# Agent attention with a gated convolution on one core: output rows issued by GpSimd in place of SyncE

## The chip, the core and the metric

The kernel runs on one core of one Trainium2 chip. The metric is the device time of one execution in microseconds, here the median of several runs. The core has five engines that run their own instruction queues: TensorE (PE; its weight loads are PEld), VectorE (DVE), ScalarE (ACT), GpSimd (POOL) and SyncE (SP). A queue runs in order: an instruction that waits holds everything behind it on its engine. Transfers are issued by an instruction on some engine's queue and then run on 16 DMA engines.

## The reference

Two stages, batch 4, sequence 12800, width 128, 49 agents:

```python
def sm(a, b):
    s = scale * (a @ b.transpose(0, 2, 1))
    s = s - s.max(-1, keepdims=True)
    e = np.exp(s)
    return e / (e.sum(-1, keepdims=True) + 1e-09)
a2k = sm(agents, k)
agent_v = a2k @ v
q2a = sm(q, agents)
x = q2a @ agent_v
# then, over the sequence
gate_pre = sum(conv_w[k] * xp[:, k:k + S, :] for k in range(5))   # xp: x, 4 zeros ahead
gate = 1.0 / (1.0 + np.exp(-gate_pre))
out = gate * (x @ w_val) @ w_out
```

## The kernel before

**Tiling.** Each batch of 12800 positions is cut into ten units of 1280 and 25 chunks of 512. A unit of k, q or v is loaded into one of eleven buffers `ld`. A unit of k gives agent scores (`key_scores`, L367 on PE), copied to `ks` by ScalarE; their maximum goes over VectorE. A unit of v gives exponentials (L459, ACT), a transpose (L377, DVE) and the accumulation `av` (L467, PE). When a batch is through, `fold_weights` turns `av` and the weights into the matrices `stat` and `wo16`, in steps on VectorE (`den`, `avT`, `mx`, `rs`, `wst`), GpSimd (`gw`, L517) and PE (L612 and others). So attention output is never formed by itself: the query side makes the softmax over agents, and the folded matrices do the rest.

**The query side.** `queries` takes a unit of q: scores on PE in one of two banks `sc`, transpose `sT` and maximum `qmx` on VectorE, subtraction `qw` on GpSimd (L703), exponential on ScalarE (L711), sums `qsm`, `qr` and product `qw` on VectorE (L716 to L725), then `pt`, the high and low halves, on ScalarE (L732) and GpSimd (L737, L747). SyncE then issues a DMA transpose of `pt` into the rows `x` (L788), and two copies that shift rows for the convolution (L837). GpSimd copies the last four columns of a segment into the next one (`halo`, L772), which has to wait for the transposes.

**The chunk.** For chunk t: `gates` (L875, L879 on PE, then tanh `th` on ACT, L888), `values` (L902, L906 on PE, `h` on DVE L915, the half-precision `hh` on ACT L921, the rest `hl` on GpSimd L926), and two chunks later `project` (L945 to L947 on PE, the copy `ob` on ACT L959). Each pair of chunks fills one of three buffers `ob` of 128 x 1024, and is sent out by one transfer (L974, SyncE). There are 53 such transfers: 48 of 512 KB, 3 of 256 KB (the last chunk of the first three batches) and 2 of 128 KB, since the very last chunk is cut in two.

**The order.** Every step is given to `Plan.add` with an engine, a time in us, what it reads and what it writes. `Plan.order` plays this through: PE keeps the order written, each other engine takes the ready step with the longest tail behind it, and the issues are written out in the order of their planned starts. Transfers ("dma") are one queue, SyncE's, and may have eight in flight (`lanes`). So a step's engine and planned time change the places of other steps too.

Of the kernel before, what the change touches and what calls it, by code (L numbers as in the profile page):

```python
# [66 lines left out]
class Plan:  # L67
# [11 lines left out]
    def add(self, engine, us, fn, reads=(), writes=(), moved=0.0, key=None, urge=0.0):  # L79
        i = len(self.steps)  # L80
        need = set()
        for x in reads:
            need |= self.wrote.get(x, set())
        for x in writes:
            need |= self.wrote.get(x, set()) | self.read.get(x, set())
        for x in reads:
            self.read.setdefault(x, set()).add(i)
        for x in writes:
            self.wrote[x], self.read[x] = {i}, set()
        self.steps.append((engine, us, fn, need, moved, key))  # L90
        self.urge.append(urge)

    def order(self):
        n = len(self.steps)
        after = [[] for _ in range(n)]
        last = None
        for i, (engine, us, fn, need, moved, key) in enumerate(self.steps):
            for j in need:
                after[j].append(i)
            if engine == "pe":  # L100
                if last is not None and last not in need:
                    after[last].append(i)
                last = i
        tail = [0.0] * n
        for i in reversed(range(n)):
            engine, us, fn, need, moved, key = self.steps[i]
            cost = us + HOP + (moved + LAND if moved else 0.0)
            if engine == "pe":
                cost = us
            tail[i] = cost + self.urge[i] + max((tail[j] for j in after[i]), default=0.0)  # L110
        engines = ("pe", "act", "dve", "pool", "dma")
        free = dict.fromkeys(engines, 0.0)
        wire = 0.0
        lanes = [0.0] * LANES
        left = [len(s[3]) for s in self.steps]
        at = [0.0] * n
        queues = {e: [] for e in engines}
        pe = [i for i, s in enumerate(self.steps) if s[0] == "pe"]
        here = 0
        for i, s in enumerate(self.steps):  # L120
            if s[0] != "pe" and not left[i]:
                queues[s[0]].append(i)
        start = [0.0] * n
        kind = None
        done = 0
        while done < n:
            best = None
            free["dma"] = max(free["dma"], wire - BACKLOG, lanes[0])
            for e in engines:
                if e == "pe":  # L130
                    if here < len(pe) and not left[pe[here]]:
                        pick, when = pe[here], max(free[e], at[pe[here]])
                    else:
                        continue
                elif queues[e]:
                    q = queues[e]
                    soon = min(max(free[e], at[i]) for i in q)
                    open_ = [i for i in q if at[i] <= soon + 0.05]
                    pick = max(open_, key=lambda i: (tail[i], -i))
                    for i in q:  # L140
                        if tail[i] > tail[pick] + 1.0 and at[i] < soon + 0.6 * self.steps[pick][1]:
                            pick = i
                    when = max(free[e], at[pick])
                else:
                    continue
                if best is None or when < best[0]:
                    best = when, e, pick
            when, e, i = best
            engine, us, fn, need, moved, key = self.steps[i]
            if e == "pe":  # L150
                here += 1
                if key != kind:
                    when += 0.12
                kind = key
            else:
                queues[e].remove(i)
            start[i] = when
            free[e] = when + us
            end = when + us + HOP
            if moved:  # L160
                wire = max(wire, when + 0.5) + moved
                end = max(wire, when + us) + LAND
                lanes = lanes[1:] + [end]
            done += 1
            for j in after[i]:
                if i in self.steps[j][3]:
                    left[j] -= 1
                    at[j] = max(at[j], end)
                    if not left[j] and self.steps[j][0] != "pe":
                        queues[self.steps[j][0]].append(j)  # L170
        self.start = start
        return sorted(range(n), key=lambda i: (start[i], i))
# [3 lines left out]
def tile_agent_attention_gated_conv(  # L176
# [9 lines left out]
    nc = tc.nc  # L186
# [61 lines left out]
    def bank():  # L248
        turn[0] += 1
        i = turn[0] % 2  # L250
        return sc[i], ("sc", i)
# [680 lines left out]
    def project(t):  # L932
        b, n0, w = chunks[t]
        x = b % 2
        wo16, oscale = wo16s[x], oscales[x]
        hh, hl = hhs[t % 3][:, 0:w], hls[t % 3][:, 0:w]
        if t >= NT - 2:
            ps, at_p = bank()
            po = ps[:, 0, 0:w]
        else:  # L940
            po, at_p = outp[:, 0:w], "out"
        scale = w / CH

        def matmuls():
            nc.tensor.matmul(out=po, lhsT=wo16[:, 0, :], rhs=hh, start=True, stop=False)  # L945
            nc.tensor.matmul(out=po, lhsT=wo16[:, 1, :], rhs=hh, start=False, stop=False)  # L946
            nc.tensor.matmul(out=po, lhsT=wo16[:, 0, :], rhs=hl, start=False, stop=True)  # L947

        add(
            "pe", 0.65 * scale, matmuls, [("hh", t % 3), ("hl", t % 3), ("wo16", x)], [at_p],  # L950
            key="c",
        )
        g = t if w == CH else NT - 1
        pair = (t // NCH * 13 + t % NCH // 2) if t < NT - 1 else (B - 1) * 13 + 12
        o = (n0 // CH % 2) * CH if w == CH else n0 - (N - CH)
        ob = obs[pair % NOB]
        add(
            "act", 0.16 + 0.46 * scale,
            lambda: nc.scalar.activation(  # L959
                out=ob[:, o : o + w], in_=po, func=AF.Copy, scale=oscale  # L960
            ),
            [at_p, ("oscale", x)], [("ob", pair % NOB, o)],
        )
        single = w < CH or n0 + w == N
        if single:
            lo, keys = o, [("ob", pair % NOB, o)]
        elif o:
            lo, keys = 0, [("ob", pair % NOB, 0), ("ob", pair % NOB, CH)]
        else:
            return  # L970
        n = o + w - lo
        add(
            "dma", 0.48,
            lambda: nc.sync.dma_start(  # L974
                out=outT[b, :, n0 + w - n : n0 + w], in_=ob[:, lo : lo + n]
            ),
            keys, [], n * 0.00125,
        )
# [61 lines left out]
    def gate_and_state(t):  # L1040
# [3 lines left out]
        "k": key_scores, "v": agent_values, "q": queries, "t": transposes,  # L1044
        "max": lambda b: step(key_max, b), "fold": lambda b: step(fold_weights, b),
        "g": gate_and_state, "a": values, "o": project,
    }
    ahead, done = 0, 0
# [56 lines left out]
```

## Time and profile before

| | |
|---|---|
| median of 3 runs | 433.42 us (433.0 to 433.8) |
| the profiled execution's own time | 432.69 us |
| its span, first to last instruction | 430.8 us |
| mean granted TensorE clock | 0.994 |
| busy: PE, DVE, ACT, POOL | 401.8, 299.0, 300.0, 227.3 us |
| bytes moved by DMA | 127.55 MB, 296 GB/s |
| read from and written to HBM | 79.25 MB, 26.21 MB |

Busy time leaves out register, branch, semaphore and transfer-issuing instructions. A row of waits has the engine and line that waited, what released it, us in total, times, and the longest. A row of the chain has start, length, and what ran. A row of the timeline has start, length, engine, line, what was done, and in brackets how long the engine stood idle before it and who ended that. Rows of "SPq" are SyncE's queue.

### The profile page before, as it was taken

How to read it: one execution, taken by the hardware profiler on the slowest of the kernel's cores; microseconds unless marked ns; L12 is line 12 of the kernel's file. 1: busy time of each engine (PE TensorE's matmuls, PEld its weight loads, DVE VectorE, ACT ScalarE, POOL GpSimd, SP SyncE). 2: the span in 40 equal slices, each digit the busy share in tenths (PEclk: the TensorE clock that was granted, in tenths of full speed). 3: DMA queues.
4: the chain of work that ended last, by engine and by line, in shares of the span. 5: the costliest groups of instructions: out<-in, count | busy, mean ns of one | idle time of the engine just before them, and what ended most of it. 6: DMA issues, size and time to landing. Idle time of an engine off the chain costs nothing.

```text
span 430.8 us, 8867 instructions
## 1 busy us (share of the span) xinstructions
PE 401.8 (93%) x3307; PEld 194.8 (45%) x3307; DVE 299.0 (69%) x567; ACT 300.0 (70%) x520; POOL 227.3 (53%) x258
## 2 busy tenths in 40 slices
PE   3878888999999999999999999999999999999995
PEld 1347333335555444444555543435555544434442
DVE  3676879877686887678666886677667787566231
ACT  2474436678986577778876676768886667777875
POOL 1002246664466765544467664662366566777543
PEclk9999989999999999999999999999999999999999
DMA  8999999999999999999999999999999996554633
GB/s 293 422 417 414 369 387 331 287 339 315 311 332 313 288 312 314 351 302 341 367 299 389 288 299 276 350 273 300 341 373 336 217 206 190 149 136 158 209 127 123
DMA packets 75365, 127.55 MB, mean 296 GB/s; under 512 B 50962, under 2 KB 51218, under 8 KB 75324
## 3 DMA queue, kind: packets, MB, share of 16 engines
q1 hardware_dynamic: 75324, 127.00, 95.6%
q8 instruction: 26, 0.43, 0.4%
q14 instruction: 15, 0.12, 0.1%
HBM read 79.25 MB, written 26.21 MB: 245 GB/s over the span
## 4 chain that ended last, share of the span: by engine, by line
PE 69%; DVE 12%; DMA 9%; ACT 5%; issue 3%; POOL 1%; SPq 0%; DVEq 0%; POOLq 0%; ACTq 0%
PE gate L875 21%; PE sc L367 14%; PE av L467 8%; PE val L902 4%; PE val L906 4%; PE gate L879 4%; PE out L945 4%; PE out L946 4%; PE out L947 4%; DMA ld<-qT 3%; DMA ld<-vP 3%; DVE h L915 2%; DMA x<-pt 2%; ACT e L459 2%; ACT th L888 1%
## 5 line engine op out<-in xcount | busy, mean ns | idle before, releaser
L926 POOL TENSOR_TENSOR hl<-h,hh 128x512 f16<-128x512 f32 (+1 forms) x101 | 117.4, 1164 | 112.6 <-ACT hh L921 111.7
L875 PE MATMUL gate<-x,stat 128*128 128x512 f16 (+1 forms) x500 | 124.2, 378 | 3.2 <-ACT th L888 3.2
L915 DVE SCALAR_TENSOR_TENSOR h<-th,val 128x512 f32<-128x512 f32 x100 | 67.7, 677 | 68.0 <-PE out L946 44.5
L367 PE MATMUL sc<-ld,ag_sb 128*32 128x320 f32 x1280 | 101.3, 448 | 10.7 <-DMA ld<-kT 8.4
L888 ACT ACTIVATE th<-gate,unscale 128x512 f32<-128x512 f32 x100 | 68.3, 683 | 22.5 <-PE gate L879 20.7
L959 ACT ACTIVATE ob<-out,oscale 128x512 f32<-128x512 f32 x98 | 67.2, 686 | 18.7 <-PE out L947 18.5
L875 PEld LDWEIGHTS <-stat 128*128 128x128 f16 x505 | 45.7, 97 | 66.3 <-issue 18.1
L921 ACT CAST hh<-h 128x512 f16<-128x512 f32 (+1 forms) x101 | 61.5, 609 | 12.8 <-DVE h L915 12.0
L703 POOL TENSOR_TENSOR qw<-sT,qmx 128x490 f32<-128x490 f32 x40 | 41.9, 1047 | 45.5 <-DVE qmx L698 45.4
L367 PEld LDWEIGHTS sc<-ld,ag_sb 128*32 128x32 f32 x1280 | 36.8, 111 | 63.5 <-issue 25.4
L393 ACT COPY ks<-sc 128x640 f32<-128x640 f32 x40 | 27.7, 692 | 35.7 <-PE sc L367 33.4
L467 PE MATMUL av<-ld,eT 128*64 128x129 f32 x800 | 49.5, 275 | 2.1 <-DMA ld<-vP 1.8
L747 POOL TENSOR_TENSOR pt<-qw,pt 128x490 f16<-128x490 f32 x40 | 44.5, 1115 | 11.8 <-ACT pt L732 11.6
L467 PEld LDWEIGHTS av<-ld,eT 128*64 128x64 f32 x800 | 43.8, 136 | 12.2 <-issue 7.2
L459 ACT ACTIVATE e<-ks,kbias 128x320 f32<-128x320 f32 x80 | 39.1, 553 | 6.5 <-DVE kbias L448 3.2
L377 DVE STREAM_TRANSPOSE eT<-e 128x640 f32<-128x640 f32 x40 | 33.6, 842 | 11.5 <-ACT e L459 5.3
L377 DVE STREAM_TRANSPOSE sT<-sc 128x640 f32<-128x640 f32 x40 | 33.4, 835 | 10.6 <-PE sc L367 10.4
L402 DVE TENSOR_REDUCE kmx<-ks 128x2 f32<-128x640 f32 x39 | 31.5, 816 | 12.0 <-ACT ks L393 12.0
L879 PE MATMUL gate<-x,stat 95*128 95x512 f16 x100 | 38.0, 380 | 0.0
L902 PE MATMUL val<-x,stat 128*128 128x512 f16 x100 | 37.8, 378 | 0.1
L906 PE MATMUL val<-x,stat 95*128 95x512 f16 x100 | 37.8, 378 | 0.0
L945 PE MATMUL out<-hh,wo 128*128 128x512 f16 x98 | 37.2, 379 | 0.0
(127 smaller groups left out, 397.2 us busy)
## 6 DMA issues: line engine op xcount, KB each, us to landing
ld<-vP SPq DMA_DIRECT2D x40, 645.0 KB
ld<-kT SPq DMA_DIRECT2D x40, 640.0 KB
ld<-qT SPq DMA_DIRECT2D x40, 640.0 KB
outT<-ob SPq DMA_DIRECT2D x48, 512.0 KB
x<-x SPq DMA_DIRECT2D x18, 375.0 KB
x<-x SPq DMA_DIRECT2D x18, 100.0 KB
outT<-ob SPq DMA_DIRECT2D x3, 256.0 KB
x<-x SPq DMA_DIRECT2D x4, 187.5 KB
```

Of the source, the lines that this page charges most:

```text
L367: nc.tensor.matmul(out=out[g * BLK : (g + 1) * BLK, j, 0:GT], lhsT=ag_sb[:, b, j * BLK : (j + 1) * BLK], rhs=src[:, g * GT : (g + 1) * GT] ...
L377: nc.vector.transpose(out=out.rearrange("p n (j i) -> p j n i", j=2), in_=in_.rearrange("p j (n i) -> p j n i", i=BLK),)
L467: nc.tensor.matmul(out=av[o : o + AP_, 0 : C + 1], lhsT=et[:, n, :], rhs=vt[:, n, :], start=(u == 0 and n < 2), stop=(u == NU - 1 and n >= ...
L875: nc.tensor.matmul(out=pg, lhsT=stat[:, k, :], rhs=x1[:, c : c + w], start=(k == 0), stop=False,)
L879: nc.tensor.matmul(out=pg, lhsT=stat[0 : TAPS * X2R, TAPS + 1, :], rhs=x2[0 : TAPS * X2R, o2 : o2 + w], start=False, stop=True,)
L888: lambda: nc.scalar.activation(out=th, in_=pg, func=AF.Tanh, scale=unscale[:, 0:1]),
L902: nc.tensor.matmul(out=pv, lhsT=stat[:, TAPS, :], rhs=x1s[(b * NCH + n0 // CH) // 5 % NX][:, PAD + o2 : PAD + o2 + w], start=True, stop=False,
L906: nc.tensor.matmul(out=pv, lhsT=stat[0 : TAPS * X2R, TAPS + 2, :], rhs=x2[0 : TAPS * X2R, o2 : o2 + w], start=False, stop=True,)
L915: lambda: nc.vector.scalar_tensor_tensor(out=h, in0=th, scalar=1.0, in1=pv, op0=ALU.add, op1=ALU.mult),
L921: "act", 0.16 + 0.42 * scale, lambda: nc.scalar.copy(out=hh, in_=h),
L926: lambda: nc.gpsimd.tensor_tensor(out=hl, in0=h, in1=hh, op=ALU.subtract),
L959: lambda: nc.scalar.activation(out=ob[:, o : o + w], in_=po, func=AF.Copy, scale=oscale),
```

## The change

The output transfer of `project` becomes a step of GpSimd with a planned time of 1.0 us, issued from GpSimd's queue. In `Plan.order` only SyncE's transfers take one of the eight places in flight.

```diff
@@ Plan.order
             if moved:
                 wire = max(wire, when + 0.5) + moved
                 end = max(wire, when + us) + LAND
-                lanes = lanes[1:] + [end]
+                if e == "dma":
+                    lanes = lanes[1:] + [end]
@@ project
         add(
-            "dma", 0.48,
-            lambda: nc.sync.dma_start(
+            "pool", 1.0,
+            lambda: nc.gpsimd.dma_start(
                 out=outT[b, :, n0 + w - n : n0 + w], in_=ob[:, lo : lo + n]
             ),
             keys, [], n * 0.00125,
```

The lines below the first hunk have numbers one higher in the changed kernel (L926 is L927 there, and so on). PE's order is the same; the orders of the others move. SyncE's queue loses its 53 output rows, and GpSimd's gains them. Three places follow.

GpSimd at the end of the program, before (`hl` are the low halves of the last chunks):

```order
L926 TENSOR_TENSOR hl_118<-h_112,hh_115 128x512
L926 TENSOR_TENSOR hl_116<-h_110,hh_113 128x512
L926 TENSOR_TENSOR hl_117<-h_111,hh_114 128x512
L926 TENSOR_TENSOR hl_118<-h_112,hh_115 128x512
L926 TENSOR_TENSOR hl_116<-h_110,hh_113 128x256
L926 TENSOR_TENSOR hl_117<-h_111,hh_114 128x256
```

and with the change:

```order
L927 TENSOR_TENSOR hl_117<-h_111,hh_114 128x512
L927 TENSOR_TENSOR hl_118<-h_112,hh_115 128x512
L975 DMA outT<-ob_120 128x1024
L927 TENSOR_TENSOR hl_116<-h_110,hh_113 128x256
L927 TENSOR_TENSOR hl_117<-h_111,hh_114 128x256
L975 DMA outT<-ob_121 128x1024
L975 DMA outT<-ob_119 128x256 x2
```

The last three transfers stand behind both of the last low halves.

VectorE in the weight fold of the second batch, before (`avT`, `mx`, `rs`, `wst` are the fold's steps, `sT` is the transpose of the next unit's scores out of the bank `sc`):

```order
L532 RECIPROCAL rs<-mx 128x1
L725 TENSOR_TENSOR qw_90<-qw_90,qr_95 128x490
L915 SCALAR_TENSOR_TENSOR h_110<-th_107,val 128x512
L583 TENSOR_SCALAR wst_123<-gw,rs 128x5x49
L564 TENSOR_REDUCE mx<-av 128x1
L568 TENSOR_SCALAR mx<-mx 128x1
L572 RECIPROCAL rs<-mx 128x1
L573 TENSOR_SCALAR wst_123<-av,rs 128x49
L558 SCALAR_TENSOR_TENSOR wst_123<-av,rs,wst_123 128x30
L558 SCALAR_TENSOR_TENSOR wst_123<-av,rs,wst_123 128x15
L558 SCALAR_TENSOR_TENSOR wst_123<-av,rs,wst_123 128x4
L377 STREAM_TRANSPOSE sT_85<-sc_133 128x2x10x32
```

and with the change:

```order
L533 RECIPROCAL rs<-mx 128x1
L584 TENSOR_SCALAR wst_123<-gw,rs 128x5x49
L916 SCALAR_TENSOR_TENSOR h_110<-th_107,val 128x512
L559 SCALAR_TENSOR_TENSOR wst_123<-gw,rs,wst_123 128x5x15 x3
L559 SCALAR_TENSOR_TENSOR wst_123<-gw,rs,wst_123 128x5x4
L378 STREAM_TRANSPOSE sT_85<-sc_133 128x2x10x32
```

The product `qw_90` and its sums went behind the transpose, and so did five short steps of the fold; the four products from `gw` went ahead of it. GpSimd's `gw` now stands ahead of a low half and not behind it. The fold of the third batch moves in the same way.

GpSimd after the fold of the third batch, before (`x_2<-x_1` is the halo copy, `qw_90<-sT_86` the subtraction of the next unit):

```order
L926 TENSOR_TENSOR hl_118<-h_112,hh_115 128x512
L737 TENSOR_SCALAR pt_96<-qw_89 128x10x30
L926 TENSOR_TENSOR hl_116<-h_110,hh_113 128x512
L747 TENSOR_TENSOR pt_96<-qw_89,pt_96 128x10x49
L926 TENSOR_TENSOR hl_117<-h_111,hh_114 128x512
L772 COPY x_2_101<-x_1_100 128x4
L703 TENSOR_TENSOR qw_90<-sT_86,qmx_88 128x490
L926 TENSOR_TENSOR hl_118<-h_112,hh_115 128x512
```

and with the change:

```order
L927 TENSOR_TENSOR hl_116<-h_110,hh_113 128x512
L975 DMA outT<-ob_121 128x1024
L927 TENSOR_TENSOR hl_117<-h_111,hh_114 128x512
L748 TENSOR_TENSOR pt_96<-qw_89,pt_96 128x10x49
L704 TENSOR_TENSOR qw_90<-sT_86,qmx_88 128x490
L738 TENSOR_SCALAR pt_96<-qw_89 128x10x30
L773 COPY x_2_101<-x_1_100 128x4
L975 DMA outT<-ob_119 128x1024
L927 TENSOR_TENSOR hl_118<-h_112,hh_115 128x512
```

The subtraction stands ahead of the halo copy now; an output and the low half stand behind it.

## Prediction

> **What bounds the kernel now.** I read the page first, then PE's waits, then a table of busy time by stage, then the chain and the timeline at the places that the table points to. The page's head and two of its engine rows:
>
> ```profile
> span 430.8 us, 8867 instructions
> ...
> PE 401.8 (93%) x3307; PEld 194.8 (45%) x3307; DVE 299.0 (69%) x567; ACT 300.0 (70%) x520; POOL 227.3 (53%) x258
> ```
>
> TensorE is busy for 401.8 of 430.8 us, so everything that this change could ever win lies in the 29.0 us in which it is idle. The table by stage (start and end, length, busy time and instruction count of PE, PEld, DVE, ACT, POOL, then clock, DMA share, GB/s) shows where those are:
>
> ```profile
> 0.00:45.00 45.00, 32.23 (x426) 19.35 (x426) 28.19 (x59) 20.28 (x36) 5.35 (x15) 1.00 0.97 388
> 45.00:75.00 30.00, 24.70 (x233) 10.83 (x237) 25.48 (x57) 16.26 (x29) 13.45 (x17) 0.94 1.02 358
> 90.00:143.00 53.00, 52.71 (x451) 27.85 (x450) 37.81 (x63) 40.88 (x75) 32.63 (x36) 1.00 1.06 315
> 143.00:150.00 7.00, 6.08 (x57) 3.10 (x56) 6.62 (x22) 5.34 (x10) 4.54 (x6) 1.00 0.98 335
> 242.00:250.00 8.00, 7.08 (x70) 3.54 (x68) 7.62 (x24) 5.50 (x10) 5.00 (x7) 1.00 1.03 377
> 253.00:267.00 14.00, 13.03 (x99) 5.79 (x97) 10.53 (x23) 9.61 (x18) 6.48 (x7) 1.00 1.08 310
> 384.00:421.00 37.00, 36.99 (x181) 16.19 (x179) 15.39 (x25) 29.64 (x49) 22.93 (x24) 1.00 0.51 166
> ```
>
> Before 75 us TensorE idles 12.77 + 5.30 = 18.07 us, and there is no output row to send yet. From 90 us on it stands at full use (52.71 of 53, 36.99 of 37) but for short gaps: 0.92 us at 143 to 150, 0.92 at 242 to 250, 0.97 at 253 to 267. Its waits name who ends them:
>
> ```profile
> PE gate L875 <- ACT th L888: 3.2, 6, 1.0
> PE sc L367 <- DVE sT L377: 2.1, 3, 0.9
> ```
>
> These two are the only kinds that recur after 75 us; none of PE's waits there is for a load or an output. The transfers that move cost SyncE this much (first the waits of its queue: us in total, times, longest; then the instructions: ns least, median, most):
>
> ```profile
> SPq L974 <- ACT ob L959: 43.3, 22, 4.4
> ...
> L974 SPq DMA_DIRECT2D outT<-ob x53: 332/401/1497, 75.6 to 427.1; - x53
> ...
> L788 SPq DMA_TRANSPOSE x<-pt x36: 1342/3943/7002, 76.2 to 400.6; - x36
> ```
>
> **Part 1: SyncE is relieved.** It loses 53 issues of 0.40 us, about 21 us, and 43.3 us of waiting for the output copies. That is off the path: TensorE does not wait for SyncE in any stage after 75 us, save through one chain, here with its start and length:
>
> ```profile
> 253.32 9.10 DMA x<-pt
> ...
> 262.84 0.19 POOL x L772
> 263.02 0.99 POOL qw L703
> ...
> 264.55 0.68 ACT th L888
> ...
> 265.27 1.24 PE gate L875 x5
> ```
>
> A DMA transpose lands late; the four-column halo copy on GpSimd waits for it; a softmax subtraction stands behind the copy, its exponential holds ScalarE, the tanh behind it is late, and TensorE loses the 0.97 us of that stage. In the changed order the subtraction goes ahead of the copy (the piece of GpSimd's order shown above), and SyncE no longer has an output between its loads there. The transpose itself comes later, since its softmax was pushed back. So the stall can go whole (−0.97) or stay (0); I take half, **−0.5**. What is late next there is the low half behind the copy, which has some slack (below).
>
> **Part 2: VectorE's order at the weight folds.** The planner gives the folds of the second and third batch another order. Rows of the first, before:
>
> ```profile
> 145.00 0.21 DVE L512 TENSOR_TENSOR avT<-av,den 128x49 f32<-128x49 f32 x1
> ...
> 146.25 1.03 POOL L517 TENSOR_TENSOR gw<-avT,moe_sb 128x245 f32<-128x245 f32 x1
> ...
> 146.74 0.68 DVE L915 SCALAR_TENSOR_TENSOR h<-th,val 128x512 f32<-128x512 f32 x1
> 147.34 0.46 DVE L583 TENSOR_SCALAR wst<-gw,rs 128x245 f16<-128x245 f32 x1
> ...
> 149.07 0.84 DVE L377 STREAM_TRANSPOSE sT<-sc 128x640 f32<-128x640 f32 x1
> 149.84 1.27 DVE L558 SCALAR_TENSOR_TENSOR wst<-gw,rs,wst 128x75 f16<-128x75 f32 x4
> ...
> 149.97 1.28 PE L367 MATMUL sc<-ld,ag_sb 128*32 128x320 f32 x16 [0.92 <-DVE sT L377]
> ```
>
> TensorE waits 0.92 us for the transpose of the scores, which frees its bank. In the new order gw follows at once on avT (145.2, to 146.27), wst takes 0.46 (to 146.75), h 0.68 (to 147.43), four products of L558 1.27 (to 148.70), and the transpose starts there in place of 149.07: 0.4 us earlier. Twice, **−0.8**. It is gone if L558 meets a low half on GpSimd, as both read two inputs from the same memory; then 0.
>
> **Part 3: GpSimd issues.** The trace has no issue by GpSimd, so I bound its price c. The same transfer takes SyncE 0.33 to 1.50 us, and the far row is the DMA transpose, 3.94 us. The nearest by engine are GpSimd's own passes over 128 partitions (xcount, busy, mean ns, idle before):
>
> ```profile
> L926 POOL TENSOR_TENSOR hl<-h,hh 128x512 f16<-128x512 f32 (+1 forms) x101 | 117.4, 1164 | 112.6 <-ACT hh L921 111.7
> ...
> L703 POOL TENSOR_TENSOR qw<-sT,qmx 128x490 f32<-128x490 f32 x40 | 41.9, 1047 | 45.5 <-DVE qmx L698 45.4
> ```
>
> I take c = 1.1 us, between these two means; the planner books 1.0. A gain below SyncE's 0.33 is excluded, as the work is not less. The SBUF — State Buffer page of the Trainium skill, section "A bandwidth-pool intuition that's wrong", has 620 ns for a DMA that GpSimd issues alone and about 3100 ns when a VectorE copy holds their common port. By the first figure the tail below would cost an estimated 0.4 us in place of 1.8 and the sum would be 432.2 on the profiled run; no run here shows either yet.
>
> 53 issues at 1.1 add 58 us to GpSimd, 227 to 285 of 431: it does not become the bound, but it has deadlines. In the last stretch:
>
> ```profile
> 419.09 0.69 ACT L959 ACTIVATE ob<-out,oscale 128x512 f32<-128x512 f32 x1 [0.34 <-PE out L947]
> ...
> 420.36 1.15 POOL L926 TENSOR_TENSOR hl<-h,hh 128x512 f16<-128x512 f32 x1 [1.23 <-ACT hh L921]
> ...
> 422.64 0.38 PE L947 MATMUL out<-hl,wo 128*128 128x512 f16 x1
> ```
>
> The output copy ends at 419.78, the issue would hold GpSimd to 420.88, and the low half behind it would end at 422.04 in place of 421.51; its product is due at 422.64. So an issue may take 0.6 us more, c up to 1.7, before TensorE waits. In the dense stages the softmax steps queue behind the issues; the tanh steps there already wait 3.2 us in six places, and I add **+0.4** (none to 1.0, a second such stall like that at 253) for issues that come in at a bad moment.
>
> **Part 4: the tail.** The last steps before:
>
> ```profile
> 424.85 1.34 POOL L926 TENSOR_TENSOR hl<-h,hh 128x256 f16<-128x256 f32 x2 [0.94 <-ACT hh L921]
> ...
> 426.47 1.22 SPq L974 DMA_DIRECT2D outT<-ob  x2
> 426.60 0.47 ACT L959 ACTIVATE ob<-sc,oscale 128x256 f32<-128x256 f32 x1 [0.21 <-PE sc L947]
> ```
>
> SyncE ends its last issue at 427.69, and 3.1 us later the span ends: landing and the closing barrier. In the new order GpSimd does both low halves first (to 426.19) and then three issues in a row: the 512 KB pair, whose data were ready at 423.75 by the row below, and two of 128 KB, the last with its data at 427.07. The last issue ends at the later of 426.19 + 3c and 427.11 + c. With c = 1.1 that is 429.49, **+1.8**; with 0.4 it is 427.5, nothing lost; with 1.5 it is 430.7, +3.0. Nothing covers this: no engine has other work there.
>
> ```profile
> 423.06 0.69 ACT L959 ACTIVATE ob<-out,oscale 128x512 f32<-128x512 f32 x1
> ```
>
> The DMA: Bandwidth & Descriptors page of the Trainium skill, section "Latency and other measured facts", gives about 1 us to the first byte for a DMA from GpSimd against 0.6 for one from SyncE. By it the estimated landing would be 0.4 us later still; I leave it out of the sum.
>
> **The sum.** −0.5 − 0.8 + 0.4 + 1.8 = +0.9 us. The profiled execution took 432.69 us, so 433.6; its kernel's median over three runs is 433.42, 0.73 more, so 434.3 as a median.
>
> **The rivals.**
> - *The issue is cheap.* With c about 0.5 the tail costs 427.69 against 427.69, nothing, and with both folds and the whole stall at 253 won (−0.8 − 0.97) the median comes to 431.7; with half of that 432.5. For it: SyncE does the same in 0.40. Against: the two means above are what a pass over 128 partitions takes the engine that would have to do it.
> - *GpSimd comes late* (slower). From c = 1.7 on the low half misses its product once per pair of chunks, and the exponentials behind GpSimd hold up the tanh. At c = 1.7 the tail ends at 431.3 (+3.6), less 0.8: 436.2. At 2.0 the tail is +4.5 and the seven pairs of the last stretch lose 0.3 each, +2.1: 439.2. For it: TensorE's gaps already come from such chains. Against: 111.7 us of GpSimd's idle time is waiting for ScalarE before a low half, so it usually is early.
> - *It cancels.* With c = 0.8 the last issue ends at 428.59, +0.9, the folds give −0.8, and the time is 433.5. The change does what it says, but SyncE's freed time was hidden anyway and the tail pays back what VectorE wins.
> - That the change is not made is excluded by the order: 53 issues stand on GpSimd's queue.
>
> **How the numbers follow.** Forecast 0.40, cheap 0.22, late 0.23, cancels 0.15. A measurement of this kernel can tell about 0.2%, 0.87 us, from no change. The forecast's own spread, c from 1.0 to 1.3 with the 253 stall whole or gone, is 433.5 to 435.4, of which I put 0.17 within 0.87 us of before and 0.23 above. With the cancelling case "same" is 0.32, "slower" 0.23 + 0.23 = 0.46, "faster" 0.22. The range runs from 432.0, which leaves out the better part of the cheap case's best end, to 437.5, which leaves out c above some 1.8. The forecast's own range is 433.5 to 435.4.
>
> **What would show it.** Right: output issues on GpSimd of 1.0 to 1.3 us; three of them in a row after the last low half; last issue near 429.5; PE's gaps at the first two folds down to 0.5 us; PE still at full use from 384 to 421. Wrong: issues of 0.5 us or 1.7 us; new waits of PE for the low half or the tanh; a first issue that takes several us and holds the low halves near 75 us; the gap at 253 to 267 unchanged or larger.

## The result and the profile after

The changed kernel takes 457.8 us (median of four, 454.3 to 462.1); the kernel before took 433.6 beside it. The ratio is 1.0524 (95% interval 1.0452 to 1.0595): 24 us slower, against a forecast of 0.9 us. In the runs below with ScalarE, with the loads on GpSimd and with the transfers and transposes alone in one ring most executions, the profiled one among them, were disturbed and some per cent longer than the fastest, so their times stand as a range without a ratio and their traces count for less.

The page of the changed kernel (span, busy time by engine, the DMA queues, the chain by engine; its line numbers are one higher than those of before):

```profile
span 455.3 us, 8840 instructions
...
PE 408.4 (90%) x3307; PEld 196.0 (43%) x3307; DVE 296.2 (65%) x567; ACT 299.4 (66%) x520; POOL 254.8 (56%) x311
...
q1 hardware_dynamic: 67692, 100.78, 78.5%
q0 software_dynamic: 7248, 26.22, 16.3%
...
PE 54%; DMA 23%; DVE 10%; POOL 4%; issue 4%; ACT 3%; SPq 1%; POOLq 0%; ACTq 0%; DVEq 0%
```

TensorE was idle for 29.0 us and is now for 46.9. The output's 26.22 MB have a queue of their own, q0; before, q1 was the only one that moved data. Transfers hold 23% of the chain; it was 9%.

The stages (columns as in the prediction's table):

```profile
0.00:45.00 45.00, 33.58 (x426) 19.95 (x426) 28.32 (x59) 20.27 (x36) 5.33 (x15) 0.96 0.97 386
...
143.00:150.00 7.00, 5.93 (x45) 3.12 (x47) 3.99 (x13) 4.38 (x8) 3.00 (x4) 1.00 1.18 263
...
205.00:250.00 45.00, 39.68 (x329) 20.63 (x327) 25.12 (x41) 27.80 (x50) 24.92 (x31) 0.92 1.04 329
250.00:300.00 50.00, 43.97 (x331) 18.79 (x329) 32.71 (x72) 30.44 (x52) 26.41 (x32) 0.97 1.07 289
300.00:350.00 50.00, 48.41 (x413) 24.75 (x411) 33.55 (x56) 38.18 (x69) 30.06 (x36) 1.00 1.05 306
350.00:400.00 50.00, 46.14 (x307) 21.21 (x306) 32.92 (x75) 32.92 (x57) 34.11 (x42) 0.97 0.78 180
```

Nothing is lost before 45 us. Most of the new idle time lies from 205 to 300 (5.3 and 6.0 us) and from 350 to 400 (3.9); before, these three stretches had 0.9, 1.0 and 1.2. The waits say for what:

```profile
POOL x L773 <- DMA x<-pt: 39.1, 9, 8.1
...
PE gate L876 <- ACT th L889: 12.7, 7, 4.5
ACT pt L733 <- DMA x<-pt: 11.5, 2, 7.4
...
PE gate L880 <- DMA x<-x: 2.2, 3, 1.1
...
PE sc L368 <- DVE sT L378: 0.7, 3, 0.3
```

Before, the halo copy waited 3.5 us for the DMA transposes in three places, now 39.1 in nine; TensorE's wait for the tanh went from 3.2 to 12.7 us. One place shows the way. The timeline of SyncE, then of ScalarE, then of TensorE:

```profile
215.41 2.48 SPq L363 DMA_DIRECT2D ld<-vP  x2
...
221.79 0.60 SPq L363 DMA_DIRECT2D ld<-kT  x1
222.48 10.17 SPq L789 DMA_TRANSPOSE x<-pt  x1
```

```profile
229.62 0.60 ACT L733 CAST pt<-qw 128x490 f16<-128x490 f32 x1
237.60 0.60 ACT L733 CAST pt<-qw 128x490 f16<-128x490 f32 x1 [7.38 <-DMA x<-pt]
238.10 0.68 ACT L889 ACTIVATE th<-gate,unscale 128x512 f32<-128x512 f32 x1
```

```profile
233.94 0.38 PE L948 MATMUL out<-hl,wo 128*128 128x512 f16 x1
238.83 2.29 PE L876 MATMUL gate<-x,stat 128*128 128x512 f16 x5 [4.52 <-ACT th L889]
...
249.41 1.25 PE L876 MATMUL gate<-x,stat 128*128 128x512 f16 x5
```

A transpose is put on SyncE's queue at 222.48, behind seven loads issued since 215.4. ScalarE needs the buffer `pt` that it reads, waits 7.38 us for it to land, and with ScalarE waits the tanh, and TensorE for 4.52 us. The five products that follow take 2.29 us in place of 1.25, as the clock has dropped too (last section). What the DMA engines did meanwhile, by queue:

```profile
q1 hardware_dynamic: 130, 0.59, 56.8%
q0 software_dynamic: 111, 0.45, 44.2%
```

This is the stretch from 230.5 to 233.0 (a row has packets, MB, and share of the 16 engines). One output holds 44% of the DMA engines while the loads, and the transpose behind them, get 57%.

### The profile page after: what moved, and what is told of

The parts are those of the page before. It is cut to its first block, busy times and chain, and to the rows that moved or that the text cites. A ratio compares the mean times of both kernels' runs of the same rounds, so it can differ in the third digit from the quotient of the medians.

```text
span 455.3 us, 8840 instructions
## 1 busy us (share of the span) xinstructions
PE 408.4 (90%) x3307; PEld 196.0 (43%) x3307; DVE 296.2 (65%) x567; ACT 299.4 (66%) x520; POOL 254.8 (56%) x311
## 2 busy tenths in 40 slices
DMA packets 74983, 127.57 MB, mean 280 GB/s; under 512 B 50962, under 2 KB 50962, under 8 KB 74940
## 3 DMA queue, kind: packets, MB, share of 16 engines
q0 software_dynamic: 7248, 26.22, 16.3%
## 4 chain that ended last, share of the span: by engine, by line
PE 54%; DMA 23%; DVE 10%; POOL 4%; issue 4%; ACT 3%; SPq 1%; POOLq 0%; ACTq 0%; DVEq 0%
PE gate L876 17%; DMA x<-pt 11%; PE sc L368 10%; PE av L468 5%; DMA x<-x 4%; PE gate L880 4%; PE val L903 3%; PE val L907 3%; PE out L946 3%; PE out L947 3%; PE out L948 3%; DMA ld<-qT 3%; DMA ld<-vP 3%; POOL hl L927 2%; DVE h L916 2%
## 5 line engine op out<-in xcount | busy, mean ns | idle before, releaser
L927 POOL TENSOR_TENSOR hl<-h,hh 128x512 f16<-128x512 f32 (+1 forms) x101 | 116.7, 1158 | 63.8 <-ACT hh L922 62.1
L876 PE MATMUL gate<-x,stat 128*128 128x512 f16 (+1 forms) x500 | 126.9, 384 | 12.7 <-ACT th L889 12.7
L368 PEld LDWEIGHTS sc<-ld,ag_sb 128*32 128x32 f32 x1280 | 36.8, 112 | 62.2 <-issue 24.9
L468 PEld LDWEIGHTS av<-ld,eT 128*64 128x64 f32 x800 | 43.7, 136 | 10.9 <-issue 6.7
L460 ACT ACTIVATE e<-ks,kbias 128x320 f32<-128x320 f32 x80 | 39.1, 553 | 6.7 <-DVE eT L378 4.3
L378 DVE STREAM_TRANSPOSE sT<-sc 128x640 f32<-128x640 f32 x40 | 33.4, 838 | 12.0 <-PE sc L368 11.7
L880 PE MATMUL gate<-x,stat 95*128 95x512 f16 x100 | 38.5, 385 | 2.2 <-DMA x<-x 2.2
L975 POOL DMA_DIRECT2D outT<-ob x53 | 31.4, 593 | 15.0 <-ACT ob L960 14.5
L948 PE MATMUL out<-hl,wo 128*128 128x512 f16 x98 | 37.1, 378 | 2.3 <-POOL hl L927 2.3
```

The source lines that it names most:

```text
L368: nc.tensor.matmul(out=out[g * BLK : (g + 1) * BLK, j, 0:GT], lhsT=ag_sb[:, b, j * BLK : (j + 1) * BLK], rhs=src[:, g * GT : (g + 1) * GT] ...
L378: nc.vector.transpose(out=out.rearrange("p n (j i) -> p j n i", j=2), in_=in_.rearrange("p j (n i) -> p j n i", i=BLK),)
L468: nc.tensor.matmul(out=av[o : o + AP_, 0 : C + 1], lhsT=et[:, n, :], rhs=vt[:, n, :], start=(u == 0 and n < 2), stop=(u == NU - 1 and n >= ...
L876: nc.tensor.matmul(out=pg, lhsT=stat[:, k, :], rhs=x1[:, c : c + w], start=(k == 0), stop=False,)
L880: nc.tensor.matmul(out=pg, lhsT=stat[0 : TAPS * X2R, TAPS + 1, :], rhs=x2[0 : TAPS * X2R, o2 : o2 + w], start=False, stop=True,)
L927: lambda: nc.gpsimd.tensor_tensor(out=hl, in0=h, in1=hh, op=ALU.subtract),
```

## The theories

A ring is here the line in which the transfers of one issuing engine wait for the DMA engines; the profile shows it as a queue (q1 is SyncE's, q0 GpSimd's).

- **Hold** (A in the first expectations): SyncE used to wait for the output copies (43.3 us in the trace of before), which kept its loads back. Freed, it issues loads early, and the transposes stand behind more of them.
- **Plan** (B): the planner's new order is bad, whoever issues.
- **Ring** (C; later also called the order theory, since the bytes only change their order): the output's bytes used to wait in SyncE's ring behind the loads. In a ring of their own they pass, and all that is in SyncE's ring, the transposes above all, lands later.

## First runs: which part of the change

**Only the issuing engine, the order of before.** The edit of the kernel before:

```diff
-            lambda: nc.sync.dma_start(
+            lambda: nc.gpsimd.dma_start(
```

> The order of every engine is that of before (the planner still books the output as SyncE's); only the engine that issues it is GpSimd. Theory A (run-ahead: SyncE, no longer held by the output copies, issues loads early, the DMA transposes stand behind more bytes and land late): slow, 445 us or more. Theory B (the planner's new order puts GpSimd's halo copy and the halves in the wrong places): about 434 us. Theory C (output bytes on a second queue slow the transposes): slow, 445 us or more.

448.7 us, ratio 1.0342 (1.0266 to 1.0419). The issuing engine alone costs 16 us; Plan cannot be the whole.

**Only the order, SyncE issues.** The edit of the changed kernel:

```diff
-            lambda: nc.gpsimd.dma_start(
+            lambda: nc.sync.dma_start(
```

> The order of every engine is that of the changed kernel (the planner still books the output as GpSimd's); only the engine that issues it is SyncE, at the output's planned place. Theory A: SyncE is held by the output copies as before, so 433 to 437 us. Theory B: as the changed kernel, about 455 us. Theory C: one queue again, 433 to 437 us.

430.75 us, ratio 0.9956 (0.9928 to 0.9984): 0.4% faster than before. Plan falls. With one and the same order, GpSimd in place of SyncE costs 27 us (some 25 by the two ratios, as the two were not run side by side). Its waits, of the program and of SyncE's queue:

```profile
POOL x L773 <- DMA x<-pt: 14.9, 4, 5.2
PE gate L876 <- ACT th L889: 3.0, 4, 1.5
...
PE sc L368 <- DVE sT L378: 0.8, 3, 0.5
```

```profile
SPq L975 <- ACT ob L960: 29.8, 16, 4.4
SPq L838 <- DMA x<-pt: 28.8, 17, 3.0
```

The last row, SyncE's row copies waiting for transposes, was 33.5 us before and is 59.4 in the changed kernel.

**ScalarE issues, the order of before.** The edit of the kernel before:

```diff
-            lambda: nc.sync.dma_start(
+            lambda: nc.scalar.dma_start(
```

> The order of before, with the output issued by ScalarE, right where its copy has just ended, so that neither SyncE nor GpSimd waits for it. Theory A: SyncE runs ahead as in the changed kernel, 445 us or more. Theory B: about 434 us, and some us more for ScalarE's issues (53 of 0.4 us are 21 us, mostly beside idle time). Theory C: slow, 445 us or more, if any second queue does it.

440.7 to 452.8 us, all four executions slower than before. So it is not GpSimd's queue alone: a second ring of another engine costs too. How much is not settled, nor what part of it ScalarE's own 53 issues have.

**The changed kernel with 16 columns of each output.** The edit of the changed kernel:

```diff
-                out=outT[b, :, n0 + w - n : n0 + w], in_=ob[:, lo : lo + n]
+                out=outT[b, :, n0 + w - n : n0 + w - n + 16], in_=ob[:, lo : lo + 16]
```

> The changed kernel, but each output transfer sends only the first 16 columns of its piece: most of the output's bytes are left out. Orders and waits are as in the changed kernel. Theory A: the loads still run ahead of the transposes, so most of the loss stays, 445 us or more. Theory B: about 455 us. Theory C (the output's bytes, interleaved from a second queue): the loss goes, 434 us or less.

430.8 us, ratio 0.995 (0.9918 to 0.9983). SyncE does not wait for the output copies here either, as in the changed kernel, and nothing is lost: Hold in its simple form falls. All 53 issues stand on GpSimd, and they cost nothing either.

## Second runs: hold or ring

**The hold kept, the bytes on GpSimd's ring.** The edit of the changed kernel:

```diff
+    held = const.tile([P, 128], F32, name="held")
...
+                nc.sync.dma_start(out=held[:, t : t + 1], in_=ob[:, lo + n - 1 : lo + n]),
                 nc.gpsimd.dma_start(
```

> The changed kernel, and ahead of each output GpSimd sends, SyncE sends one column of the same output buffer into a spare tile (512 bytes), so that SyncE's queue is held by the output copies at the same places as in the run that kept SyncE and took the new order (430.8 us), while the bytes leave by GpSimd's ring. Hold theory (the copies used to hold SyncE's loads back, and a transfer that stands behind fewer loads lands earlier): the loss goes, 430 to 436 us. Ring theory (a second ring takes every other turn of the DMA engines, so SyncE's ring with the transposes runs at half speed meanwhile): the loss stays, 450 us or more. Between the two, 437 to 449, means that both have a part.

455.6 to 475.0 us, ratio 1.0589 (1.0465 to 1.0713). SyncE's queue:

```profile
SPq L838 <- DMA x<-pt: 37.7, 17, 3.6
SPq L977 <- ACT ob L961: 21.8, 14, 5.5
```

SyncE waits for the output copies in 14 places, 21.8 us, nearly as in the run with SyncE and the new order (16, 29.8), and the loss stays whole. Hold falls as the main cause. The 53 small transfers of SyncE are an addition of this run, and no run shows what they cost alone.

**No hold, one ring.** The changed kernel, with the output put on SyncE's queue at the next output copy:

```diff
-            lambda: nc.gpsimd.dma_start(
+            lambda: waiting.append(lambda: nc.sync.dma_start(
```

> The changed kernel's order, the output issued by SyncE, but put on its queue only one chunk later (at the next output copy), so that SyncE no longer waits for the copy that it sends; all bytes stay in one ring. Hold theory: SyncE runs ahead as in the changed kernel, 445 us or more, and no more than 10 us of waiting for output copies on SyncE. Ring theory: as with SyncE before, 430 to 435 us.

433.9 us, ratio 1.0036 (1.0001 to 1.0071). The edit missed its aim: SyncE still waits 24.9 us for output copies. It says only that one ring is not slow with the outputs a chunk later.

**The halo copy planned later.** The edit of the changed kernel:

```diff
-                end = max(wire, when + us) + LAND
+                end = max(wire, when + us) + LAND + (6.0 if us == 1.4 else 0.0)
```

> The changed kernel, but the planner books 6 us more for a DMA transpose to land, so that what waits for one (the halo copy on GpSimd above all, which holds everything behind it) is put later in the queues. Both theories of why the transposes land late allow that the late halo copy only passes the loss on: if the queue behind it is how TensorE comes to wait, 434 to 445 us and GpSimd's waits for transposes under 15 us. If TensorE waits for the transposes' rows themselves: 450 us or more.

453.4 us, ratio 1.0439 (1.0349 to 1.0529). The halo copy now waits 8.1 us, and TensorE waits for the rows themselves (`PE gate L880 <- DMA x<-x`: 10.0 us in five places). The halo copy only passes the loss on; where it is spared, the rows are late.

**Eight load buffers in place of eleven.** The edit of the changed kernel:

```diff
-NLOAD = 11
+NLOAD = 8
```

> The changed kernel with 8 load buffers in place of 11, so that SyncE can run ahead by fewer loads. Hold theory: fewer bytes stand ahead of the transposes, 440 to 450 us, unless the loads themselves come late (then TensorE waits for loads at the key, value and query scores). Ring theory: no better than the changed kernel, 455 us or more.

448.3 us, ratio 1.0343 (1.0265 to 1.0421), some 9 us better than the changed kernel. This is inside what Hold forecast and against Ring's "no better". Fewer loads ahead of the transposes have a part, then, though most of the loss is still there; the planner's order changes too, so the part of each is open.

## Third runs: how much of a second ring, and where

**Every other pair of chunks by GpSimd.** The edit of the changed kernel:

```diff
-            lambda: nc.gpsimd.dma_start(
+            lambda: (nc.gpsimd if pair % 2 else nc.sync).dma_start(
```

> The changed kernel's order, every other pair of chunks sent by GpSimd and the rest by SyncE, at the same planned places: a dose of the second ring without any work left out. Ring theory: about half of the loss, 438 to 450 us, and SyncE's waits of its row copies for transposes between the 28.8 us of one ring and the 59.4 us of the changed kernel. If the loss needs all of the output on a second ring: 430 to 435 us.

441.4 us, ratio 1.0216 (1.0188 to 1.0244); the row copies wait 43.5 us for transposes, between 28.8 and 59.4. Half of the output on the second ring has less than half of the loss (2.2% against 5.2%).

**Half of the columns, all by GpSimd.** The edit of the changed kernel:

```diff
-                out=outT[b, :, n0 + w - n : n0 + w], in_=ob[:, lo : lo + n]
+                out=outT[b, :, n0 + w - n : n0 + w - n // 2], in_=ob[:, lo : lo + n // 2]
```

> The changed kernel, each transfer sending only the first half of its columns: half of the output's bytes are left out. Bytes on the second ring as the dose: between the 430.8 us with 16 columns and the 457 us with all, 436 to 447 us. If it is the number of transfers or rings and not the bytes: 450 us or more.

430.7 us, ratio 0.9975 (0.9962 to 0.9987). This missed all that was expected: about as many bytes went by the second ring as in the run above, and nothing is lost. The difference is the other half, 13 MB that this run does not move at all. So there is no fixed price per byte. SyncE's row copies still wait 47.6 us for transposes here, as long as in the run above, but the halo copy only 1.6 us (20.8 above). The waits of the row copies alone do not foretell the time, then; we read the two runs as saying that a late transpose costs where an engine on TensorE's path waits for it.

**The last batch alone by GpSimd.** The edit of the changed kernel:

```diff
-            lambda: nc.gpsimd.dma_start(
+            lambda: (nc.gpsimd if b == B - 1 else nc.sync).dma_start(
```

> The changed kernel's order, outputs of the last batch alone sent by GpSimd (14 transfers, a quarter of the bytes), the rest by SyncE. The loads end about when that batch begins. Ring theory: a second ring costs only while SyncE's ring is full of loads, so 430 to 434 us. If each output byte on the second ring costs the same wherever it is: a quarter of the loss, 436 to 438 us.

432.6 us, ratio 1.0012 (0.9987 to 1.0036): a quarter of the output on a second ring, after the loads, costs 1.8 us against the same order with SyncE throughout. In its trace 0.7 of that is the end of the program (5.0 us behind TensorE's last product, 4.3 with SyncE). This is what Ring forecast.

**The loads on GpSimd, the outputs on SyncE.** The edit of the changed kernel:

```diff
-        add("dma", 0.4, lambda: nc.sync.dma_start(out=dst, in_=src), (), [("ld", i)], 1.57)
+        add("dma", 0.4, lambda: nc.gpsimd.dma_start(out=dst, in_=src), (), [("ld", i)], 1.57)
...
-            lambda: nc.gpsimd.dma_start(
+            lambda: nc.sync.dma_start(
```

> The changed kernel's order, with outputs back on SyncE and instead all 120 loads of k, q and v issued by GpSimd: the transposes no longer stand behind loads in a ring, but share the DMA engines with another ring that is nearly always full. If two rings take turns packet by packet, a transpose of small packets next to loads of 5 KB packets gets slower: 460 us or more, transposes 10 us or more from issue to landing. If standing behind the loads is what costs: the transposes land in under 5 us, and the time is 425 to 435 us, unless GpSimd's own queue, held by loads that wait for buffers, is late (then GpSimd's waits say so).

493.6 to 534.3 us. GpSimd is late too (its halo copy waits 56.1 us), so the time does not belong to the rings alone. The transposes' own landing is nearer to the question, from issue to landing:

```profile
DMA to landing us min/median/max: 3.4/12.8/26.1
```

This row has only 4 of the 36 transposes, as the profile could not tell the landing of the others. By the packet records (end of the next section) the 36 take a median of 7.1 us, no less than the 7.1 of the run with SyncE and the new order, a mean of 10.9 against 6.9, and at most 27.5 against 11.7. So with no load ahead of it in its ring a transpose was not quicker in this trace, and some were far slower.

## Fourth runs: does mixing cost the DMA engines time?

The shares of the queues times the span give 414 us of DMA work before (96.1% of 430.8) and 434 in the changed kernel (95.3% of 455.3). That looked like a bound, and a new theory: the same bytes cost more when two rings are mixed. Four kernels move the transfers without any computation:

```diff
+    for i in range(120):
...
+            nc.sync.dma_start(
+                out=ld[i % NLOAD][:, 0:UNIT], in_=src[b, :, u * UNIT : (u + 1) * UNIT]
+            )
+        if i >= 6 and i % 2 == 0 and sent < 48:
+            n0 = sent % 12 * 1024
+            out_from.dma_start(
+                out=outT[sent // 12, :, n0 : n0 + 1024], in_=ld[(i - 5) % NLOAD][:, 0:1024]
+            )
...
+        if i >= 6 and i % 3 == 0 and turned < 36:
+            nc.sync.dma_start_transpose(
...
+                in_=pts[turned % 3].rearrange("p n r -> p (n r)"),
+            )
```

`out_from` is SyncE or GpSimd; the transposes are left out in the second pair.

> The transfers alone, with all computation left out: the 120 loads, 48 outputs of 512 KB (each sends a load buffer five loads after it was filled) and 36 DMA transposes, all issued by SyncE. Nothing waits for a transpose. From the engine times of the profile before (240 us for loads, 66 for outputs, 99 for transposes) 400 us, if the DMA engines alone set it.

> The same transfers, the outputs issued by GpSimd. Engine-time theory (the same bytes cost the DMA engines more when two rings are mixed, and the kernel is bound by them): 10 to 30 us over the run with one ring, and a longer mean packet of the outputs. Order theory (the outputs only pass the loads and transposes, which then land later, and the kernel waits for these): the same time within 1%, since nothing here waits for a transpose.

> Loads and outputs alone, without the transposes, all issued by SyncE: about 305 us by the engine times of the profile before.

> Loads and outputs alone, the outputs issued by GpSimd. Engine-time theory: if loads and outputs disturb each other, 5 to 15 us over the run with one ring; if it takes the transposes' small packets, the same within 1% here and the difference only with transposes. Order theory: the same within 1%.

Without transposes the time is the same, 255.3 us in one ring and 255.2 in two: loads and outputs do not slow each other by being in two rings. With transposes the times do not settle it: 304.0, 319.6, 324.2 and 326.9 us in one ring, 314.6 to 317.5 in two. The engines' busy time did not rise, though: 336 us in the trace with one ring (105.7% of 317.8) and 331 in that with two (105.1% of 314.9). The engine-time theory finds no support, but for the transposes it is not excluded. The reading of a DMA share near 1 as a bound does fall: the transfers that keep the engines "busy" for 414 us take 304 to 327 when nothing waits for them (the row copies and five small outputs aside).

What differs is when each lands. Median us from issue to landing without transposes, in the run with one ring, then in that with two:

```profile
ld<-vP SPq DMA_DIRECT2D x40, 645.0 KB, 11.8
...
outT<-ld SPq DMA_DIRECT2D x48, 512.0 KB, 11.5
```

```profile
ld<-vP SPq DMA_DIRECT2D x40, 645.0 KB, 16.9
...
outT<-ld POOLq DMA_DIRECT2D x48, 512.0 KB, 7.0
```

The bytes take the same time in all, but the outputs land 4.5 us sooner and the loads 5.1 us later: the second ring passes the first. With transposes, again one ring and then two:

```profile
ld<-vP SPq DMA_DIRECT2D x40, 645.0 KB, 7.6
...
ld<-qT SPq DMA_DIRECT2D x40, 640.0 KB, 7.9
outT<-ld SPq DMA_DIRECT2D x48, 512.0 KB, 7.7
x<-pt SPq DMA_TRANSPOSE x36, 9.8
```

```profile
ld<-vP SPq DMA_DIRECT2D x40, 645.0 KB, 8.1
...
ld<-qT SPq DMA_DIRECT2D x40, 640.0 KB, 9.1
outT<-ld POOLq DMA_DIRECT2D x48, 512.0 KB, 7.5
x<-pt SPq DMA_TRANSPOSE x36, 11.8
```

The outputs gain 0.2 us here, the loads lose 0.5 to 1.3, the transposes 2.0.

**Are 2 us on the transposes enough?** The new order with SyncE throughout, one ring, and a load more ahead of each transpose:

```diff
+                    nc.sync.dma_start(out=more[g % 2], in_=qT[b, :, 0:1152]),
                     nc.sync.dma_start_transpose(
```

> The run that kept SyncE and took the new order (430.8 us), with one load more, of 576 KB into a spare buffer, put on SyncE's queue ahead of each of the 36 DMA transposes: no second ring, but each transpose stands behind 1.4 us more of transfer (by the 255 us of 102 MB in the loads-and-outputs run). Order theory (a transpose that lands 1.5 to 2 us later is what costs): 440 us or more, with GpSimd's waits for transposes well over the 14.9 us of the run without. If late landings are hidden and a second ring costs in another way: 429 to 434 us.

466.5 us, ratio 1.0778 (1.0723 to 1.0834), with the changed kernel's own marks:

```profile
POOL x L773 <- DMA x<-pt: 37.8, 9, 11.7
...
PE gate L881 <- ACT th L894: 14.1, 10, 3.1
...
PE gate L885 <- DMA x<-x: 4.9, 3, 2.0
```

One load more ahead of every transpose, an estimated 1.4 us, costs 36 us with no second ring at all. The run also moves 21 MB more (148.80 against 127.57 MB), which delays other transfers too, so not all of it need be the transposes'.

**Transposes further forward in SyncE's queue, two rings.** The edit of the changed kernel:

```diff
-LANES = 8
+LANES = 3
```

> The changed kernel, planned with 3 transfers of SyncE in flight in place of 8, so that the transposes stand 1 to 4 loads further forward in SyncE's queue; the outputs stay with GpSimd. Order theory: the transposes land earlier and part of the loss goes, 438 to 450 us. If the place among the loads is without weight: 455 us or more.

455.3 us, ratio 1.051 (1.0438 to 1.0581). A miss for Ring: the place among the loads did not matter in this form.

**How late the transposes are in the kernels themselves.** The profile tells no landing there, but the packet records of the kept traces do. A transpose is 1280 packets of 256 bytes, in SyncE's ring. (The first 512 packets of this size come before any transpose.) Taken in order of their start, they give the time from a transpose's issue to the end of its last packet. For the two runs of the transfers alone this gives medians of 9.3 and 11.3 us, each 0.5 less than the landing above. The mean of all 36 in each kernel:

| run | mean, us | time, us |
|---|---|---|
| 16 columns | 4.3 | 430.8 |
| half of the columns | 6.2 | 430.7 |
| no hold, one ring | 6.6 | 433.9 |
| before | 6.7 | 433.6 |
| SyncE, new order | 6.9 | 430.75 |
| last batch by GpSimd | 6.9 | 432.6 |
| GpSimd, order of before | 7.2 | 448.7 |
| every other pair | 7.3 | 441.4 |
| hold kept | 7.4 | 455.6 to 475.0 |
| three in flight | 7.7 | 455.3 |
| eight load buffers | 7.8 | 448.3 |
| a load more ahead | 8.0 | 466.5 |
| the change | 8.1 | 457.8 |
| halo copy later | 9.3 | 453.4 |

The six runs without a loss have at most 6.9, the eight with one at least 7.2. With half of the columns the transposes are earlier than with SyncE, which is why that run lost nothing, as far as these records tell. Two things do not fit: ScalarE's run has 6.9 and loses, and among the runs with a loss the mean does not give its size. A stalled kernel also issues its transposes at other moments, so a part of the lateness can be an effect of the loss.

## Why the prediction was wrong

**The step that failed is Part 1**: "That is off the path: TensorE does not wait for SyncE in any stage after 75 us, save through one chain", priced at −0.5 us. It asked what SyncE's queue loses, and not what the transfer's bytes do in a ring of their own. Measured with the order kept, the move of the bytes costs 16 us (448.7 against 432.5), and with the new order 27 (457.8 against 430.75). With the new order the transposes took a mean of 8.1 us from issue to last packet in place of 6.9. The trace of before had the warning: that one chain was a transpose of 9.10 us, and SyncE's row copies waited 33.5 us in 19 places for transposes. The prediction counted one transpose, had it start later, and put nothing in its sum for transposes that take longer. The rest of the step was not wrong: in the run with SyncE and the new order the stretch from 253 to 267 has 13.80 us of products in place of 13.03, so the reorder took most of that stall away; in the changed kernel it has 12.20. Of the 26.9 us of span between the changed kernel and its order with SyncE, 21.5 are idle time of TensorE (46.9 against 25.4) and 5.4 the same products taking longer (408.4 against 403.0 us busy), most of it at a lower granted clock (a mean of 0.977 against 0.988).

On the DMA: Bandwidth & Descriptors page of the Trainium skill, section "Queues, rings and completion order", each DMA engine takes turns between the rings that have work, a packet at a time. The stretch above agrees: 130 packets of SyncE's queue and 111 of GpSimd's. The same page's section "Rules for kernel authors" says that spreading transfers over several issuing engines only saves sequencer time; for the bytes this case agrees (255.2 us from two rings, 255.3 from one). That the 5.2% lost here come from what lands later, and not from bandwidth, is our reading of the runs above.

**Part 2 was right and small.** TensorE's wait for the transpose of the scores fell from 2.1 to 0.7 us, by 1.4 (forecast 0.8). With SyncE and the new order the stretch from 143 to 150 is full (7.00 of 7 us, 6.08 before); in the changed kernel it has 5.93, with other waits in it. The new order by itself is worth 1.9 us, and the version that has it with SyncE is the fastest of those that leave nothing out, 0.9956 of before.

**Part 3 was mis-sized, without effect.** The issue took a mean of 0.593 us, not 1.1:

```profile
L975 POOL DMA_DIRECT2D outT<-ob x53 | 31.4, 593 | 15.0 <-ACT ob L960 14.5
```

It is near the 620 ns that the SBUF — State Buffer page of the Trainium skill, section "A bandwidth-pool intuition that's wrong", has for a DMA that GpSimd issues alone; nothing like the 3100 ns beside it came in 53 issues (longest 0.745 us). The +0.4 for issues at a bad moment is not to be seen: with 16 columns the issues are all there and the time is 430.8.

**Part 4 came near by luck.** From TensorE's last product to the end there are 6.6 us (448.71 to 455.3), before 4.2 (426.56 to 430.8): +2.4 against +1.8. But the issues end only 0.3 us later behind that product; from the last issue to the end it takes 5.2 us in place of 3.1:

```profile
448.47 1.65 POOL L975 DMA_DIRECT2D outT<-ob  x3
```

By the prediction's own sum an issue of 0.59 us costs just these 0.3 us; the rest is a longer end, which it put at nothing. With 16 columns it takes 5.2 us too, so the last transfers' bytes do not set it. Most of it is GpSimd's closing drain instruction, 5.04 us in the changed kernel and 4.96 with 16 columns; with the last batch alone by GpSimd the drain is 3.44 and the end 3.6. What the drain waits for, no run shows.

**The rivals.** "The issue is cheap" had its condition nearly met (0.59 us for 0.5) and came out 26 us wrong, "It cancels" 24; "GpSimd comes late" had the right sign, but GpSimd was late because its halo copy waited for transposes, not because of the issues. No rival had the second ring, so the range had nothing of this size in it.

**What stays open.** It is shown that moving the output's bytes to a second ring, and not the issues or the order, brings the loss, that a second ring passes what waits in the first, and that the engines then wait for transposes. That the transposes' lateness accounts for all of the 24 us is argued: the one run that delays them in a single ring also moves 21 MB more, and eight load buffers did better than Ring allowed. How 1 or 2 us become 24 is not taken apart: the new order makes it worse (16 to 24 us) though it is better in one ring, and the run with the transposes further forward did not help.

## What to carry to other kernels

Ask of a moved transfer not only which queue its issue leaves, but which ring its bytes leave: behind other transfers it was the one that waited, in a ring of its own it passes them, and the one to look at is the transfer with a dependent on the critical path. Look in the trace of before for engines that wait for such transfers, even where TensorE does not lose by it yet. A DMA share near 1 is no proof of a bound: move the bytes without the computation to know.

## What was not expected of the hardware

After a gap of TensorE of 4.5 us the granted clock was 0.50 for 4.2 us (the third number from the end of a row; the rows are the stretches before the gap, the gap, and behind it):

```profile
230.00:234.00 4.00, 4.00 (x45) 2.63 (x42) 2.63 (x4) 0.22 (x1) 3.35 (x4) 1.00 1.15 402
234.00:238.80 4.80, 0.32 (x2) 0.04 (x1) 0.00 (x0) 1.20 (x3) 0.96 (x2) 0.75 1.11 190
238.80:243.00 4.20, 4.17 (x10) 1.47 (x10) 1.15 (x2) 2.36 (x4) 2.27 (x3) 0.50 1.01 373
243.00:246.00 3.00, 3.00 (x17) 1.28 (x19) 2.16 (x6) 1.93 (x4) 1.15 (x2) 0.96 0.99 288
```

So a stall of 4.5 us costs an estimated 2.1 us more in products at half speed (half of 4.2). The TensorE: Matmul & The Clock Gate page of the Trainium skill, section "What's actually happening", has half the clock after about 3.4 us of idling, and the trace agrees. With transfers issued by GpSimd the program stayed open for 5.2 us behind the last issue, against 3.1 with SyncE; its closing drain took 5.04 us after 53 issues, 3.43 after 27 and 3.44 after 14.
